# Attention weights' sums in an attention and mixture-of-experts kernel: last full key tile summed by TensorE, narrow pieces added two key tiles at once on GpSimd

## The chip, the core and the metric

The kernel runs on one core of one Trainium2 chip. The metric is device time in microseconds of one execution. TensorE does the matrix products (PE in the profile; PEld is its loading of weights), VectorE is DVE, ScalarE is ACT, GpSimd is POOL, and SyncE (SP) issues the DMAs.

## What is computed

There are 4 batches of 8 heads, 768 queries and keys a head, 64 dimensions. A query sees only the keys of its own cluster. The output of attention goes through 8 experts, with gates that are normalised 8 times over rows and columns.

```python
mask = q_assign[:, :, :, None] == k_assign[:, :, None, :]
scores = scale * np.matmul(q, k.transpose(0, 1, 3, 2))
scores = np.where(mask, scores, -1000000000.0)
scores = scores - np.max(scores, axis=-1, keepdims=True)
attn = np.exp(scores)
attn = attn / (np.sum(attn, axis=-1, keepdims=True) + 1e-09)
out = np.matmul(attn, v)
...
for e in range(E):
    h = np.maximum(x @ w1[e], 0.0)
    out += P[:, e:e + 1] * (h @ w2[e])
```

The change concerns `np.sum(attn, axis=-1)`, the sums by which the weights are divided.

## The kernel before

The kernel has two stages: attention, to about 530 us of the trace, and the experts, from there to the end at 2337.6 us. Heads are worked on in 16 pairs. The weights of a head lie with keys on the 128 partitions and queries along the row. There are six key tiles of 128 keys, and the 768 queries are cut at `N0` = 512. `CHUNKS` lists nine chunks a head, in three groups of three: key tile u with queries 0 to 511, key tile u+1 with queries 0 to 511, and then both key tiles with queries 512 to 767, side by side in one 512-wide tile. Chunk 7 (`NCH - 2`) is the last key tile with queries 0 to 511; chunk 8 is the last of all.

For each chunk, `max_chunk` (TensorE, line 733, then a VectorE maximum, line 737) and `max_rows` find the rows' maxima. In `max_rows` the maxima are rounded and split by ScalarE and GpSimd (lines 753 to 761), transposed on TensorE (line 766), copied by ScalarE (line 771) and moved by DMA into the operands of the next products. `exp_chunk` computes the scores on TensorE (lines 803 and 804, two PSUM buffers), and ScalarE turns them into the weights `pe` (line 810), in a ring of `PB` = 14 buffers. GpSimd then adds the weights into `psum`, a running sum over key tiles (line 829): ten adds a head, five of them 512 wide and five 256 wide. `values` multiplies the weights with V (line 862). `norm`, once a pair, adds `psum` up over the partitions with four products by ones (line 900), each into its own strip of 32 PSUM partitions, takes reciprocals and scales the output.

All products of lines 862, 900 and 1004 are in float32, and each leaves two matmul records in the trace.

The order of all engines' instructions is set by a planner when the program is built. Processes such as `exp_chunk` yield an engine and an estimated cost; the planner picks the next by key and start, and every engine then runs its instructions in that order. Tokens stand for buffers: `t_pe` has `PB` of them, and `release` gives one back when the add of a chunk (`ev["s", n, c]`) and its product with V are planned. Some steps may go to either of two engines: `split_part` subtracts (line 609) on VectorE or GpSimd, and one step of `assign_pair` (line 647) likewise. The experts' stage is planned apart, after attention. Its preparation of weights starts while the last pair is still under way (lines 1228 to 1251, 1353).

Of the kernel before, what the change touches and what calls it, by code (L numbers as in the profile page):

```python
# [8 lines left out]
F32 = mybir.dt.float32  # L9
# [5 lines left out]
ALU = mybir.AluOpType  # L15
# [7 lines left out]
P = 128  # L23
# [137 lines left out]
def attn_moe_kernel(  # L161
# [11 lines left out]
    nc = tc.nc  # L173
    B, H, S, D = q.shape
# [7 lines left out]
    SCALE = 1.0 / float(D) ** 0.5  # L182
    G = 4
    NA, NB = 3, 4
    PB = 14
    N0 = 512
    SPANS = ((0, N0), (N0, S))

# [12 lines left out]
    ones = const.tile([P, P], F32, name="ones")  # L201
# [11 lines left out]
    Q = 32  # L213
# [11 lines left out]
    PE, ACT, DVE, POOL, SP = "PE", "ACT", "DVE", "POOL", "SP"  # L225
# [114 lines left out]
    with ExitStack() as actx:  # L340
        nat = actx.enter_context(tc.tile_pool(name="nat", bufs=2))
        brief = actx.enter_context(tc.tile_pool(name="brief", bufs=1))
        work = actx.enter_context(tc.tile_pool(name="work", bufs=2))
# [27 lines left out]
        ps = misc_tile()  # L371
# [17 lines left out]
        bufs = {nm: [] for nm in NSET}  # L389
# [60 lines left out]
        NCH = len(CHUNKS)  # L450
# [56 lines left out]
        heads = {}  # L507
# [278 lines left out]
        def exp_chunk(n, c):  # L786

            p, y = divmod(n, 2)
            yield ev["rows", n]
            for to in (("qH", "kL"), ("kH", "qL"))[y]:  # L790
                yield ev["cross", p, to]
            if c:
                yield ev["begun", n, c - 1]
            yield t_s
            yield PE, 0.436, 0.107, 0.213
            t = heads[n]
            ev["begun", n, c].set(plan)
            i0, ni, a, z = CHUNKS[c]
            ps = ps_s.tile([P, 512], F32, name="exp_ps")
            for x in range(ni):  # L800
                ki = slice((i0 + x) * P, (i0 + x + 1) * P)
                o = ps[:, x * (z - a) : (x + 1) * (z - a)]
                nc.tensor.matmul(o, t["k1"][:, ki], t["q1"][:, a:z], start=True, stop=False)  # L803
                nc.tensor.matmul(o, t["k2"][0:98, ki], t["qa"][0:98, a:z], start=False, stop=True)  # L804
            if c == NCH - 1:
                ev["e", n].set(plan)
            yield t_pe
            yield ACT, 0.5
            pe = t["pe", c] = work.tile([P, ni, z - a], F32, name="pe", bufs=PB)
            nc.scalar.activation(pe, ps.rearrange("p (x c) -> p x c", x=ni), AF.Exp, scale=SCALE)  # L810
            t_s.put(plan)
            ev["p", n, c].set(plan)

            if c == 0:
                yield t_sum
                t["sum"] = work.tile([P, S], F32, name="psum", bufs=4)
                t["add"] = {}
            st, old = t["sum"], t["add"]
            if ni == 1:
                parts = [pe[:, 0]]  # L820
            else:
                parts = [pe[:, 0], pe[:, 1]]
            for part in parts:
                if a not in old:
                    old[a] = part
                    continue
                n_ = z - a
                yield POOL, 0.09 + n_ * 0.0019
                nc.gpsimd.tensor_tensor(out=st[:, a:z], in0=old[a], in1=part, op=ALU.add)  # L829
                old[a] = st[:, a:z]  # L830
            ev["s", n, c].set(plan)

        def release(p, c):

# [53 lines left out]
        def norm(p):  # L888
# [2 lines left out]
            b, h = divmod(n, H)  # L891
            for x in range(2):
                yield ev["s", n + x, NCH - 1]
            yield t_norm
            yield t_x
            yield PE, 0.75, 0.107, 0.64
            HS = S // 2
            ps = misc_tile()
            for g in range(4):
                nc.tensor.matmul(  # L900
                    ps[g * Q : (g + 1) * Q, 0:HS], ones[:, 0:Q], heads[n + g // 2]["sum"][:, g % 2 * HS : (g % 2 + 1) * HS], start=True, stop=True
                )
            for x in range(2):
                t_sum.put(plan)
            yield ACT, 0.48
            sc = work.tile([P, HS], F32, name="sc")
# [835 lines left out]
```

## Time and profile before

| | us |
|---|---|
| median of 3 runs (2338.98 to 2342.15) | 2341.17 |
| the profiled execution | 2339.39 |
| its span in the trace | 2337.6 |
| TensorE busy over the span | 2267.1 |
| GpSimd busy over the span | 1431.6 |
| VectorE busy over the span | 1873.1 |

The profile's page gives busy time by engine over the whole span, but the stages differ, so windows by stage are read beside it. A row of a group gives its line, engine, operation, tiles and shapes, its count, its busy time, the mean of one, and the idle time of the engine before it with what ended that. The chain of waits is followed back from the last instruction: at each step to what released it. A busy TensorE counts a matmul to the modelled end of its pipeline, so it isn't the same as a TensorE that streams at its peak.

### The profile page before, as it was taken

Reading aid. Unit: us, or ns where it says so; the run is one execution under the profiler, and the core shown is the slowest. Engines: PE = TensorE matmul, PEld = TensorE weight load, DVE = VectorE, ACT = ScalarE, POOL = GpSimd, SP = SyncE. Lnnn points to the kernel's source line nnn. Section 1 sums busy time; section 2 is a strip of 40 time slices with the busy share of each in tenths; the row PEclk is TensorE's granted clock in tenths of the full one; section 3 lists DMA queues with packets and bytes.
Section 4 is the critical chain, followed back from the end, with each engine's and each line's share of the span. In section 5 each row is a group of like instructions: output and inputs, shape, how many; then the busy total and the mean of one; then the engine's idle time right before and its main releaser. Section 6 shows DMA issues by size and latency. Waiting matters only on the chain.

```text
span 2337.6 us, 43307 instructions
## 1 busy us (share of the span) xinstructions
PE 2267.1 (97%) x16244; PEld 1611.5 (69%) x16244; DVE 1873.1 (80%) x3586; ACT 1155.6 (49%) x2313; POOL 1431.6 (61%) x1452
## 2 busy tenths in 40 slices
PE   7999999986999999999999999999999999999999
PEld 4555556543667777777777777777777777777777
DVE  7787777758988897789778877887797789777776
ACT  4555555565555554445444454545354545444432
POOL 4777888888846674646555573748274746556432
PEclk7999999997999999999999999999999999999999
DMA  6554454424424252243415242623252343414142
GB/s 162 138 143 112 101 126 100 123 96 169 145 94 147 84 167 87 93 140 111 131 49 176 86 142 61 199 83 114 84 168 79 101 129 122 131 49 131 50 141 82
DMA packets 172659, 271.49 MB, mean 116 GB/s; under 512 B 62904, under 2 KB 98848, under 8 KB 171936
## 3 DMA queue, kind: packets, MB, share of 16 engines
q1 hardware_dynamic: 172448, 268.72, 38.3%
q8 instruction: 127, 2.08, 0.4%
q14 instruction: 84, 0.69, 0.1%
HBM read 216.19 MB, written 23.59 MB: 103 GB/s over the span
## 4 chain that ended last, share of the span: by engine, by line
PE 85%; DVE 7%; POOL 3%; ACT 1%; issue 1%; DMA 1%; SPq 0%; DVEq 0%; ACTq 0%; POOLq 0%
PE a_ps L1434 20%; PE a_ps L1617 14%; PE ac_ps L1617 12%; PE c_ps L1617 10%; PE c_ps L1434 10%; PE b_ps L1434 5%; PE av_ps L862 4%; PE max_ps L733 3%; PE exp_ps L803 2%; POOL psum L829 2%; PE exp_ps L804 2%; DVE mrt L737 2%; PE misc_ps L591 1%; DVE vsum L542 1%; PE misc_ps L900 1%
## 5 line engine op out<-in xcount | busy, mean ns | idle before, releaser
L1617 PEld LDWEIGHTS <-h 128*128 128x128 f16 x8064 | 789.9, 98 | 198.2 <-issue 14.1
L1434 PEld LDWEIGHTS <-wa 128*128 128x128 f16 x5376 | 526.9, 98 | 281.1 <-issue 25.2
L1474 POOL TENSOR_TENSOR h<-s,h 128x384 f16<-128x384 f32 x126 | 126.0, 1000 | 530.0 <-ACT h L1472 527.6
L1463 ACT ACTIVATE h<-c 128x384 f16<-128x384 f32 x384 | 200.4, 522 | 436.0 <-DVE c L1457 434.4
L1617 PE MATMUL a_ps<-wb,h 128*128 128x256 f16 x3072 | 377.2, 273 | 3.4 <-DVE acc L1651 1.4
L1617 PE MATMUL ac_ps<-wb,h 128*128 128x256 f16 x2688 | 366.7, 273 | 2.6 <-DVE acc L1651 1.9
L1657 DVE SCALAR_TENSOR_TENSOR acc<-a_ps,gates,acc 128x256 f32<-128x256 f32 x472 | 220.7, 479 | 93.2 <-PE a_ps L1617 91.1
L1617 PE MATMUL c_ps<-wb,h 128*128 128x256 f16 x2304 | 284.9, 274 | 4.6 <-DVE acc L1653 3.4
L829 POOL TENSOR_TENSOR psum<-psum,pe 128x512 f32<-128x512 f32 (+1 forms) x256 | 265.8, 1058 | 36.9 <-ACT pe L810 30.1
L1474 POOL TENSOR_TENSOR h<-c,h 128x384 f16<-128x384 f32 x253 | 247.2, 989 | 48.7 <-ACT h L1472 39.8
L1465 DVE SCALAR_TENSOR_TENSOR h<-c,h 128x384 f16<-128x384 f32 x384 | 259.3, 678 | 5.1 <-ACT h L1463 5.0
L737 DVE TENSOR_REDUCE mrt<-max_ps 128x1 f32<-128x512 f32 (+1 forms) x288 | 189.9, 683 | 45.2 <-PE max_ps L733 43.5
L1657 DVE SCALAR_TENSOR_TENSOR acc<-ac_ps,gates,acc 128x256 f32<-128x256 f32 x412 | 197.1, 479 | 35.0 <-PE ac_ps L1617 32.6
L1657 DVE SCALAR_TENSOR_TENSOR acc<-c_ps,gates,acc 128x256 f32<-128x256 f32 x352 | 159.4, 478 | 79.3 <-PE c_ps L1617 78.8
L810 ACT ACTIVATE pe<-exp_ps 128x512 f32<-128x512 f32 x288 | 165.3, 596 | 96.5 <-PE exp_ps L804 70.4
L1454 ACT ACTIVATE c<-a_ps 128x384 f32<-128x384 f32 x256 | 124.9, 488 | 154.0 <-PE a_ps L1434 153.2
L1472 ACT CAST h<-c 128x384 f16<-128x384 f32 x256 | 128.1, 509 | 81.2 <-DVE c L1548 80.7
L1474 POOL TENSOR_TENSOR h<-h,h 128x384 f16<-128x384 f32 x125 | 141.8, 1134 | 35.7 <-PE c_ps L1617 23.9
L862 PE MATMUL av_ps<-pe,vn 128*64 128x512 f32 (+1 forms) x768 | 137.2, 500 | 0.0
L733 PE MATMUL max_ps<-kX,qX 96*128 96x256 f32 (+1 forms) x384 | 123.6, 388 | 8.0 <-DVE mrt L737 5.1
L804 PE MATMUL exp_ps<-qX,kX 98*128 98x256 f32 (+1 forms) x384 | 126.5, 342 | 0.0
L1454 ACT ACTIVATE h<-a_ps 128x384 f32<-128x384 f32 x128 | 62.7, 490 | 118.0 <-PE a_ps L1434 118.0
(478 smaller groups left out, 3938.6 us busy)
## 6 DMA issues: line engine op xcount, KB each, us to landing
raw<-in_moe_w SPq DMA_DIRECT2D x120, 512.0 KB
qn<-in_q SPq DMA_DIRECT2D x16, 384.0 KB
kn<-in_k SPq DMA_DIRECT2D x16, 384.0 KB
vn<-in_v SPq DMA_DIRECT2D x8, 768.0 KB
qX<-qH SPq DMA_DIRECT2D x32, 192.0 KB
kX<-kH SPq DMA_DIRECT2D x32, 192.0 KB
xd<-xT SPq DMA_DIRECT2D x4, 1536.0 KB
xqB<-xd SPq DMA_DIRECT2D x16, 384.0 KB
```

The source lines that it names most:

```text
L733: nc.tensor.matmul(ps[:, y * (z - a) : (y + 1) * (z - a)], t["qa"][0:96, i * P : (i + 1) * P], t["k2"][0:96, a:z], start=True, stop=True)
L737: nc.vector.tensor_reduce(out=t["mr"][:, i0 : i0 + ni, ni - 1], in_=ps.rearrange("p (x c) -> p x c", x=ni), axis=AX, op=ALU.max)
L804: nc.tensor.matmul(o, t["k2"][0:98, ki], t["qa"][0:98, a:z], start=False, stop=True)
L829: nc.gpsimd.tensor_tensor(out=st[:, a:z], in0=old[a], in1=part, op=ALU.add)
L862: nc.tensor.matmul(av[o, a:z], vn[:, i, :], heads[t]["pe", c][:, i - i0], start=(i == 0), stop=False, skip_group_check=True)
L1434: nc.tensor.matmul(ps[:, 0:HB], wt[:, w_, a, c, :], xv[:, x_, c, :], start=(n in (0, 1, 5) and s_ == 0), stop=(s_ == len(steps) - 1), skip ...
L1454: nc.scalar.activation(t, ps[:, 0:HB], func, scale=KAPPA)
L1463: nc.scalar.activation(t[:, 0], c, AF.Relu)
L1465: nc.vector.scalar_tensor_tensor(out=t[:, 1], in0=c, scalar=0.0, in1=t[:, 0], op0=ALU.max, op1=ALU.subtract)
L1474: by(w).tensor_tensor(out=t[:, 1], in0=c, in1=t[:, 0], op=ALU.subtract)
L1617: nc.tensor.matmul(view(m, i), t[:, a_, i * P : (i + 1) * P], w[:, b_, x, :], start=(opens and n == 0 and i in (0, 2)), stop=(n == 5), ski ...
L1657: nc.vector.scalar_tensor_tensor(out=to, in0=src, scalar=gate[b, e][:, ti : ti + 1], in1=to, op0=ALU.mult, op1=ALU.add)
```

## The change

Three things change. Chunks of the narrow kind (queries 512 to 767 of two key tiles) are no longer added as two 256-wide pieces, but as one 512-wide piece, so that `psum` grows to 1024 columns, of which the last 512 hold two partial sums side by side. Chunk 7 is no longer added on GpSimd at all: `norm` adds it with products of its own, from the weights themselves. So a head has six 512-wide adds in place of ten, and a pair has 12 products by ones in place of 4, with twice the columns in each strip of 32 partitions. `PB` goes from 14 to 12 to make room for the wider `psum`, and the buffer of chunk 7 is given back only after `norm`'s products.

```diff
-    PB = 14
+    PB = 12
...
-                t["sum"] = work.tile([P, S], F32, name="psum", bufs=4)
+                t["sum"] = work.tile([P, N0 + 2 * (S - N0)], F32, name="psum", bufs=4)
...
-            if ni == 1:
-                parts = [pe[:, 0]]
-            else:
-                parts = [pe[:, 0], pe[:, 1]]
-            for part in parts:
+            for part in [pe.rearrange("p x c -> p (x c)")] * (c != NCH - 2):
...
-                n_ = z - a
+                n_ = ni * (z - a)
                 yield POOL, 0.09 + n_ * 0.0019
-                nc.gpsimd.tensor_tensor(out=st[:, a:z], in0=old[a], in1=part, op=ALU.add)
-                old[a] = st[:, a:z]
-            ev["s", n, c].set(plan)
+                nc.gpsimd.tensor_tensor(out=st[:, a : a + n_], in0=old[a], in1=part, op=ALU.add)
+                old[a] = st[:, a : a + n_]
+            if c != NCH - 2:
+                ev["s", n, c].set(plan)
...
-            yield PE, 0.75, 0.107, 0.64
+            yield PE, 1.4, 0.107, 1.3
...
             for g in range(4):
-                nc.tensor.matmul(
-                    ps[g * Q : (g + 1) * Q, 0:HS], ones[:, 0:Q], heads[n + g // 2]["sum"][:, g % 2 * HS : (g % 2 + 1) * HS], start=True, stop=True
-                )
+                t, (a, z) = heads[n + g // 2], (g % 2 * HS, (g % 2 + 1) * HS)
+                own = []
+                if a < N0:
+                    m = min(z, N0)
+                    own = [(t["sum"][:, a:m], a, m), (t["pe", NCH - 2][:, 0, a:m], a, m)]
+                if z > N0:
+                    m, L = max(a, N0), S - N0
+                    own += [(t["sum"][:, y + m : y + z], m, z) for y in (0, L)]
+                for i, (v_, fa, fz) in enumerate(own):
+                    nc.tensor.matmul(
+                        ps[g * Q : (g + 1) * Q, fa - a : fz - a], ones[:, 0:Q], v_,
+                        start=(i == 0), stop=(i == len(own) - 1), skip_group_check=True,
+                    )
             for x in range(2):
+                ev["s", n + x, NCH - 2].set(plan)
                 t_sum.put(plan)
```

On TensorE, at the end of the last pair, the products by ones stood so before, between the last products with V and the transposes of the sums (line 911):

```order
L862 MATMUL av_ps<-pe,vn 64x512 x4
L862 MATMUL av_ps<-pe,vn 64x256 x4
L870 MATMUL av_ps<-nht_202,ve 128x512
L870 MATMUL av_ps<-nht_202,ve 128x256
L900 MATMUL misc_ps<-psum,ones 32x384 x4
L911 MATMUL misc_ps<-ident,sc 128x128 x3
```

Now, at the same place, where line 907 is the products by ones and 859, 867 and 920 are the lines around them:

```order
L867 MATMUL av_ps<-nht_202,ve 128x256
L907 MATMUL misc_ps<-psum,ones 32x384
L907 MATMUL misc_ps<-pe,ones 32x384
L907 MATMUL misc_ps<-psum,ones 32x128
L907 MATMUL misc_ps<-pe,ones 32x128
L907 MATMUL misc_ps<-psum,ones 32x256 x2
L907 MATMUL misc_ps<-psum,ones 32x384
L907 MATMUL misc_ps<-pe,ones 32x384
L907 MATMUL misc_ps<-psum,ones 32x128
L907 MATMUL misc_ps<-pe,ones 32x128
L907 MATMUL misc_ps<-psum,ones 32x256 x2
L920 MATMUL misc_ps<-ident,sc 128x128 x3
```

The first two go to the first strip of 32 partitions, the next four to the second, and so on: products of one strip now stand behind each other, where each had a strip of its own before.

On GpSimd, in the middle of attention, this stood before between the roundings of the maxima of two heads that follow each other (line 755; 756 and 761 belong to it):

```order
L755 TENSOR_SCALAR mm_195<-mr_2426 128x6
L756 TENSOR_TENSOR mm_195<-mr_2426,mm_195 128x6
L829 TENSOR_TENSOR psum<-psum,pe 128x512
L761 TENSOR_SCALAR flags_214<-mr_2426 128x6
L829 TENSOR_TENSOR psum<-psum,pe 128x512
L829 TENSOR_TENSOR psum<-psum,pe 128x256 x4
L829 TENSOR_TENSOR psum<-psum,pe 128x512 x2
L755 TENSOR_SCALAR mm_196<-mr_2543 128x6
```

And now, between the same two heads' roundings (the adds are line 825):

```order
L755 TENSOR_SCALAR mm_195<-mr_2410 128x6
L756 TENSOR_TENSOR mm_195<-mr_2410,mm_195 128x6
L761 TENSOR_SCALAR flags_214<-mr_2410 128x6
L825 TENSOR_TENSOR psum<-psum,pe 128x512 x3
L825 TENSOR_TENSOR psum<-pe 128x512 x2
L755 TENSOR_SCALAR mm_196<-mr_2564 128x6
```

Eight adds between the two roundings have become five.

At the end of attention, the first steps of the experts' weights (lines 1243, now 1252) stood on GpSimd behind 16 of the last pair's 20 adds; the last rows were:

```order
L829 TENSOR_TENSOR psum<-psum,pe 128x512
L829 TENSOR_TENSOR psum<-psum,pe 128x256
L1243 TENSOR_TENSOR sums<-raw 128x256
L1243 TENSOR_TENSOR sums<-sums,raw 128x256
L1243 TENSOR_TENSOR sums<-raw 128x256 x2
L829 TENSOR_TENSOR psum<-psum,pe 128x512
L829 TENSOR_TENSOR psum<-psum,pe 128x256 x3
L1251 TENSOR_TENSOR wa<-raw,wa 128x256
```

Now they begin behind 3 of the last pair's 12 adds:

```order
L825 TENSOR_TENSOR psum<-pe 128x512 x2
L825 TENSOR_TENSOR psum<-psum,pe 128x512
L1252 TENSOR_TENSOR sums<-raw 128x256
L1252 TENSOR_TENSOR sums<-sums,raw 128x256
L825 TENSOR_TENSOR psum<-psum,pe 128x512
L1252 TENSOR_TENSOR sums<-raw 128x256
L825 TENSOR_TENSOR psum<-psum,pe 128x512
L1252 TENSOR_TENSOR sums<-raw 128x256
L825 TENSOR_TENSOR psum<-psum,pe 128x512
L825 TENSOR_TENSOR psum<-pe 128x512 x2
L825 TENSOR_TENSOR psum<-psum,pe 128x512 x4
L1260 TENSOR_TENSOR wa<-raw,wa 128x256
```

The planner has also moved twelve of the subtractions of line 609 from GpSimd to VectorE (GpSimd had 32 and has 20: three 512 wide and nine 256 wide fewer), three steps of line 647 from VectorE to GpSimd, and three casts from ScalarE to VectorE. From the first product of the experts' stage to the end, TensorE's order is the same as before.

## Rows read from the trace of the kernel before

**Rows 1.** The page: busy time by engine; the chain that ended last.

```profile
PE 2267.1 (97%) x16244; PEld 1611.5 (69%) x16244; DVE 1873.1 (80%) x3586; ACT 1155.6 (49%) x2313; POOL 1431.6 (61%) x1452
...
PE 85%; DVE 7%; POOL 3%; ACT 1%; issue 1%; DMA 1%; SPq 0%; DVEq 0%; ACTq 0%; POOLq 0%
```

**Rows 2.** Windows by stage: length, then each engine's busy us, granted clock, DMA.

```profile
60.00:490.00 430.00, 418.44 (x2421) 247.93 (x2419) 321.32 (x575) 239.32 (x509) 343.08 (x403) 1.00 0.46 114
490.00:530.00 40.00, 33.59 (x171) 15.86 (x168) 14.66 (x21) 25.03 (x43) 35.38 (x37) 0.91 0.49 173
...
560.00:700.00 140.00, 120.44 (x867) 86.36 (x868) 131.72 (x264) 76.42 (x150) 95.82 (x85) 0.95 0.37 124
700.00:2330.00 1630.00, 1628.21 (x12490) 1221.89 (x12489) 1329.43 (x2574) 770.08 (x1530) 907.58 (x870) 1.00 0.36 112
```

**Rows 3.** Groups by line and shape, 40 to 540 us: the adds and subtractions.

```profile
L829 POOL TENSOR_TENSOR psum<-psum,pe 128x512 f32<-128x512 f32 x128 | 165.8, 1304 | 28.1 <-ACT pe L810 24.3 <-ACT mm L753 1.1 <-ACT mt L771 0.5
...
L829 POOL TENSOR_TENSOR psum<-psum,pe 128x256 f32<-128x256 f32 x128 | 102.2, 811 | 8.7 <-ACT pe L810 5.8
...
L829 POOL TENSOR_TENSOR psum<-pe 128x512 f32<-128x512 f32 x32 | 42.2, 1317 | 39.7 <-ACT pe L810 39.4
...
L829 POOL TENSOR_TENSOR psum<-pe 128x256 f32<-128x256 f32 x32 | 25.5, 806 | 6.2 <-ACT pe L810 6.0
...
L609 DVE TENSOR_TENSOR kL<-kn,kH 128x512 fp32r<-128x512 f32 x8 | 8.1, 1012 | 0.1
...
L609 DVE TENSOR_TENSOR qL<-qn,qH 128x256 fp32r<-128x256 f32 x3 | 2.4, 792 | 0.0
```

**Rows 4.** TensorE's timeline at the first pair's sums: start, length, line, tiles, count.

```profile
76.31 0.85 PE L900 MATMUL misc_ps<-psum,ones 128*32 128x384 f32 x8
77.09 0.74 PE L733 MATMUL max_ps<-kX,qX 96*128 96x512 f32 x3
```

**Rows 5.** TensorE's timeline at two other groups of products in strips.

```profile
70.26 0.51 PE L627 MATMUL misc_ps<-qn,cm 128*32 128x384 f32 x1
70.27 0.51 PE L627 MATMUL misc_ps<-kn,cm 128*32 128x384 f32 x1
...
70.61 0.49 PE L627 MATMUL misc_ps<-qn,cm 128*32 128x384 f32 x1
...
326.85 1.93 PE L1004 MATMUL misc_ps<-xT,wg 128*32 128x256 f32 x24
328.71 0.73 PE L733 MATMUL max_ps<-kX,qX 96*128 96x512 f32 x3
```

**Rows 6.** The chain of waits, 40 to 490 and 490 to 545 us: shares, longest pieces.

```profile
by line: PE av_ps L862 18.5%; PE max_ps L733 13.4%; PE exp_ps L803 10.7%; PE exp_ps L804 8.9%; POOL psum L829 8.3%; DVE mrt L737 7.2%; PE misc_ps L591 3.3%; issue 2.7%; DVE vsum L542 2.5%; PE misc_ps L900 2.4%; PE misc_ps L956 1.9%; ACT pe 
...
202.75 6.50 POOL psum L829 x7
...
by line: POOL psum L829 24.3%; issue 9.3%; ACT pe L810 7.4%; PE misc_ps L1004 6.7%; DMA xqB<-xd 6.2%; POOL xqB L328 5.1%; PE misc_ps L900 4.6%; PE c_ps L1434 3.8%; PE a_ps L1434 3.5%; POOL sums L1243 2.9%; DVE sums L1282 2.7%; PE exp_ps L80
```

**Rows 7.** Waits, 40 to 530 us: who waited for whom, total us, times, longest.

```profile
ACT mt L771 <- PE misc_ps L766: 24.5, 16, 2.7
PEld exp_ps L803 <- ACT pe L810: 14.4, 34, 1.5
...
ACT pe L810 <- POOL psum L829: 11.6, 7, 3.8
...
PEld misc_ps L766 <- POOL mm L756: 4.7, 5, 1.7
```

**Rows 8.** GpSimd's timeline at the end of attention.

```profile
498.66 3.48 POOL L829 TENSOR_TENSOR psum<-pe 128x512 f32<-128x512 f32 x2 [0.26 <-ACT pe L810]
502.10 11.60 POOL L829 TENSOR_TENSOR psum<-psum,pe 128x512 f32<-128x512 f32 x11
```

**Rows 9.** TensorE's timeline at the end of attention: gaps in brackets with what ended them.

```profile
506.30 0.39 PE L803 MATMUL exp_ps<-qL,kH 128*128 128x256 f32 x1 [1.07 <-ACT pe L810]
...
520.58 0.83 PE L900 MATMUL misc_ps<-psum,ones 128*32 128x384 f32 x2 [0.82 <-POOL psum L829]
```

More of the change, by code (lines that the diff above doesn't have):

```diff
@@ L893, in norm @@
                 yield ev["s", n + x, NCH - 1]
+                yield ev["p", n + x, NCH - 2]
             yield t_norm
             yield t_x
-            yield PE, 0.75, 0.107, 0.64
+            yield PE, 1.4, 0.107, 1.3
             HS = S // 2
```

## The prediction

> **What bounds the kernel now.** I read the page first, then windows by stage, then the chain of waits and the waits of the attention stage, and last the timelines at the places where the adds stand on the chain. The page says that TensorE is busy for 97% of the span and carries 85% of the chain, GpSimd 3% [rows 1]. That is an average over two stages. From 700 us on TensorE is busy 1628.21 of 1630 us, and from 560 to 700 us VectorE is busy 131.72 of 140 [rows 2]. The change touches neither, and TensorE's order there is the old one, so whatever attention gains or loses reaches the end unchanged. I look for the result before 530 us alone.
>
> From 60 to 490 us TensorE is busy 418.44 of 430 us, GpSimd 343.08, VectorE 321.32 [rows 2]. So TensorE bounds attention too, but narrowly: it idles 11.6 us there, and its in-order queue hides short waits in the ends of matmuls. GpSimd comes next, at 80%. The chain from 40 to 490 us runs through the adds for 8.3% of the time, and from 490 to 545 us for 24.3% [rows 6]: 0.083 x 450 = 37 us and 0.243 x 55 = 13 us. At 202.75 us seven adds stand in a row on it, ahead of the rounding of a head's maxima, for which TensorE waits. The question is thus whether freeing the second engine is worth more than loading the first.
>
> **The change, part by part.**
>
> GpSimd loses work. Before, all 320 adds take 165.8 + 102.2 + 42.2 + 25.5 = 335.7 us [rows 3]. After, each head has two first adds, which read two weight tiles (chunks 1 and 5), and four that read `psum`, all 512 wide: 64 x 1.317 + 128 x 1.304 = 251 us. That is 84.5 us less, or 5.3 us a pair. It is free only where GpSimd is waited for.
>
> TensorE gains work. A pair's sums took 0.78 us from their first start to the next instruction, 77.09 - 76.31, in eight records [rows 4]. Each strip of 32 partitions had 384 columns; now each has 768: 384 + 384 in the first and third, 128 + 128 + 256 + 256 in the second and fourth. What this costs depends on whether strips still run beside each other when the products of one strip stand behind each other in the queue. At 70.26 us products by line 627 stand in the order q, k, q, k, each with two records. Their first records start within 0.02 us, and the second records 0.35 us after them [rows 5]: the second half of the first product didn't hold up the first half of the next strip's. At 326.85 us 24 records of 256 columns in three strips are through in 1.86 us (328.71 - 326.85), eight rounds of 0.23 us [rows 5]. One record after another would take 24 x 0.23 = 5.6 us. So a blocked strip lets others pass, for at least the one or two products that stand there. I take strips side by side: the extra 384 columns a strip cost two more records of 0.35 us, +0.70 us a pair, 16 x 0.70 = +11.2 us, nearly all of it on the path, since TensorE has so little idle time. No row shows three products of a strip queued ahead of another strip; if strips then ran one by one, the price is the second rival's.
>
> The Trainium skill says otherwise: "TensorE: Matmul & The Clock Gate", Part 3 (packing small matmuls), has matmuls start and end in program order, with only weight loads pulled ahead. By that the four strips would hardly overlap, as in the second rival. The starts at 70.26 us [rows 5] speak against it, but they show a shallower queue than the new one.
>
> What freeing GpSimd gives back in the steady part (60 to 490 us) no row states. Its lower bound is nothing: TensorE is already 97% busy, and twelve subtractions move to VectorE, 3 x 1.012 + 9 x 0.792 = 10 us more there [rows 3]. Its upper bound is the idle 11.6 us, or more if waits hidden in matmul ends go too. The waits that a queue of adds can cause are: TensorE for the rounded maxima, 4.7 us in 5 times, ScalarE for weight buffers that an add still holds, 11.6 us, then TensorE for ScalarE's exponentials, 14.4 us, and ScalarE for the transposes behind the rounding, 24.5 us [rows 7]. They overlap, and most of what ScalarE waits never reaches TensorE. I take 7 us, over half the idle time, since the adds fall by a quarter and the eight adds between two roundings shown in the order become five.
>
> At the end of attention GpSimd is the bound. From 498.66 us it adds almost without a gap, 11 adds in 11.60 us from 502.10 on [rows 8]; TensorE meanwhile waits 1.07 us for exponentials and at 520.58 us 0.82 us for the last adds [rows 9]. The last pair's adds shrink by the 5.3 us above. Nothing back is the lower bound, 5.3 us the upper; I take 5.3, because GpSimd hardly pauses there. The steps of the experts' weights that now stand ahead of most of these adds take GpSimd's time at another place, not more of it; I cost that move at nothing, covered by VectorE, which is busy only 14.66 of 40 us there [rows 2].
>
> The ring of 12 `pe` buffers: what waits is ScalarE's exponential, behind which its whole queue stands, and then TensorE. Chunk 7's buffer is now held until the sums, chunk 2's until the add of chunk 5. Against that, GpSimd runs less behind. I cost it at nothing; its cover is the slack of GpSimd, and without it the third rival follows.
>
> Sum: +11.2 - 7 - 5.3 = -1.1 us against the profiled execution, 2339.39 us, so 2338.3 us; I say 2338. That execution lies 1.8 us under the median of the runs shown, 2341.17. The bounds of this case: steady part 0 to 11.6 back, the end 0 to 5.3 back, give 2339.4 + 11.2 - 16.9 = 2334 to 2351; as its own range I take 2331 to 2346, as both ends together are unlikely and some hidden waits may go.
>
> About 0.2%, 4.7 us, is what a measurement of this kernel can tell from no change: below 2336.5 is faster, above 2345.9 slower.
>
> **The rivals.**
>
> First, faster: GpSimd's queue is the true pace. The chain holds 37 + 13 = 50 us of adds [rows 6], more than TensorE's idle time, because a late rounding or buffer delays a whole head and TensorE fills in with other work that is due later. If half of these 50 us go, 2339.4 + 11.2 - 25 = 2325 us; if all, 2300. For it: GpSimd's 343 of 430 us and the seven adds in a row. Against: TensorE's 97%.
>
> Second, much slower: strips don't run side by side when their products queue behind each other. Then a product of 384 columns takes 0.70 us, of 256 0.46 and of 128 0.23, and only the last record of a strip overlaps the next strip's first: some 4.5 us a pair where it was 0.78, 3.7 x 16 = +60 us, and with the same 12.3 us back 2387 us. It decides as soon as a strip's first record starts after the strip before it has ended. Against it stand the starts at 70.26 and the 1.86 us at 326.85 [rows 5]; for it only that the queue ahead is longer.
>
> Third, slower: twelve buffers are too few. ScalarE's wait for buffers that adds hold, 11.6 us now [rows 7], doubles, passes to TensorE through the two score buffers, and eats what GpSimd gives back: 2339.4 + 11.2 = 2351 us. It decides where that wait grows past some 20 us. Against it: the adds now cost GpSimd 5.3 us a pair less, so buffers are freed sooner.
>
> **How the numbers follow.** Forecast 0.44 (faster 0.14, same 0.24, slower 0.06), first rival 0.27 (all faster), second 0.10 (all slower), third 0.19 (same 0.02, slower 0.17). So faster 0.41, same 0.26, slower 0.33. The range goes from 2316, into the first rival's far half, to 2360, past the third's; it leaves out the second (0.10) and perhaps 0.07 at the fast end.
>
> **What would show it.** In the changed kernel's profile: adds of 250 us in 192; GpSimd near 260 us busy in the same 430; the products by ones 1.4 to 1.6 us from first start to next instruction, with the second strip starting beside the first (else the second rival); the chain's share of adds from 40 to 490 us well under 8.3%, and TensorE's idle time there some 5 us; attention's last products by ones within a few us of 520.58; ScalarE's wait for adds not above 11.6 us (else the third rival). The forecast is wrong at its root if the time past 700 us moves, or if the pairs come closer together by over 1 us each, which TensorE's 97% doesn't allow without hidden waits.

## The result

The changed kernel takes 2351.81 us (median of 7 runs, 2347.27 to 2358.42) where the kernel before takes 2341.2 us (7 runs, 2338.98 to 2343.22): 10.6 us more, a ratio of 1.005 with a 95% interval of 1.0035 to 1.0065. It is slower, by more than the 0.2% that counts here, and 13.8 us above the 2338 forecast. It lies inside the range, but on the other side. The execution that was profiled took 2357.73 us, 6 us over the median of its seven, so its trace holds somewhat more than there is to explain on average; where that lies is said below. One run of e_fewer (2391.56 us) and one of the kernel before (3841.72 us) lie far above the others of their kernels and are left out of the differences below.

The page of the kernel after: busy time by engine, then the chain that ended last (they answer to [rows 1]).

```profile
PE 2289.5 (97%) x16500; PEld 1635.9 (69%) x16500; DVE 1877.1 (80%) x3598; ACT 1154.7 (49%) x2310; POOL 1338.5 (57%) x1315
...
PE 88%; DVE 7%; DMA 1%; issue 1%; ACT 1%; POOL 1%; SPq 1%; DVEq 0%; ACTq 0%; POOLq 0%
```

Windows by stage of the kernel after, in the columns of [rows 2]: length, busy us of PE, PEld, DVE, ACT, POOL, granted clock, DMA.

```profile
60.00:490.00 430.00, 419.94 (x2542) 257.56 (x2539) 310.81 (x562) 228.30 (x487) 245.05 (x266) 0.98 0.46 114
490.00:530.00 40.00, 37.79 (x204) 22.09 (x202) 22.97 (x34) 26.73 (x49) 27.79 (x28) 0.96 0.25 83
...
700.00:2330.00 1630.00, 1627.77 (x12467) 1219.63 (x12466) 1332.75 (x2574) 784.29 (x1562) 915.12 (x875) 1.00 0.35 111
```

GpSimd fell from 343 to 245 us busy in 60 to 490 us. TensorE is as full as it was: it idles 10.1 us there, where it idled 11.6. The experts' stage is the old one. So it is attention that got longer. The adds by shape (they answer to [rows 3]; the columns are busy us, mean ns, idle time before them):

```profile
L825 POOL TENSOR_TENSOR psum<-psum,pe 128x512 f32<-128x512 f32 x128 | 165.9, 1307 | 62.9 <-ACT pe L810 54.3 <-ACT mm L753 6.0 <-ACT rt L948 0.9
...
L825 POOL TENSOR_TENSOR psum<-pe 128x512 f32<-128x512 f32 x64 | 83.6, 1314 | 101.2 <-ACT pe L810 88.7 <-DMA qX<-mt 5.0 <-DMA nht<-mt 5.0
```

165.9 + 83.6 = 249.5 us in 192 adds: the relief of GpSimd is what the change promised, 86 us. ScalarE's wait for adds, 11.6 us in [rows 7], is down to 0.4 us. GpSimd is the one that waits, from 40 to 530 us (the list's first row: total us, times, longest), and the adds are gone from the chain of 40 to 490 us, where [rows 6] had 8.3%:

```profile
POOL psum L825 <- ACT pe L810: 142.9, 65, 8.6
```

```profile
by line: PE av_ps L859 20.8%; PE max_ps L733 14.7%; PE exp_ps L803 12.3%; PE exp_ps L804 10.2%; PE misc_ps L907 6.3%; DVE mrt L737 4.5%; PE misc_ps L591 3.5%; issue 2.1%; PE misc_ps L627 2.1%; PE misc_ps L965 2.0%; DMA rrow<-rt 1.7%; ACT pe
```

TensorE's timeline at the first pair's sums of the kernel after (answers to [rows 4]; start, length, line, tiles, count):

```profile
74.79 0.51 PE L907 MATMUL misc_ps<-psum,ones 128*32 128x384 f32 x3
75.04 0.27 PE L907 MATMUL misc_ps<-pe,ones 128*32 128x128 f32 x1
...
75.46 0.49 PE L907 MATMUL misc_ps<-pe,ones 128*32 128x384 f32 x1
...
75.78 0.49 PE L907 MATMUL misc_ps<-pe,ones 128*32 128x384 f32 x1
...
75.94 0.49 PE L907 MATMUL misc_ps<-pe,ones 128*32 128x384 f32 x1
...
76.26 0.49 PE L907 MATMUL misc_ps<-pe,ones 128*32 128x384 f32 x1
...
76.70 0.50 PE L733 MATMUL max_ps<-kX,qX 96*128 96x512 f32 x1
```

The burst lasts 76.70 - 74.79 = 1.91 us from its first start to the next instruction; before it was 0.78. That is +1.13 us a pair, +18.1 us for 16 pairs, where the prediction had +0.70 and +11.2. Why, the rows with 384 columns of chunk 7's weights (`pe`) show. The first head's two records start at 75.46 and 75.78, the second head's at 75.94 and 76.26: 0.48 us later. The strips of one head run side by side, but the second head's begin only when the first head's are partly through. Fourteen of the sixteen bursts are 1.91 us long; one at half clock takes 3.59, and behind the last one TensorE waits for ScalarE.

The first and the last burst start at 74.79 and 538.49 us, 463.7 us apart; before, at 76.31 and 517.62, 441.3 us apart. Fifteen bursts account for 17.0 of the 22.4 us. The clock adds to it in this execution (columns as in the windows above):

```profile
131.00:134.00 3.00, 1.74 (x8) 0.86 (x6) 1.50 (x4) 2.59 (x6) 1.30 (x1) 0.96 0.61 146
...
134.00:144.00 10.00, 9.91 (x42) 6.81 (x43) 5.03 (x9) 3.12 (x8) 3.96 (x4) 0.50 0.28 73
...
290.80:294.20 3.40, 3.40 (x16) 1.47 (x14) 2.19 (x4) 1.65 (x4) 2.20 (x2) 0.50 0.27 60
```

And TensorE's timeline at the start of that stretch:

```profile
131.63 0.46 PE L965 MATMUL misc_ps<-rrow,pick 4*128 4x512 f32 x1 [0.43 <-DMA rrow<-rt]
...
134.09 1.22 PE L733 MATMUL max_ps<-kX,qX 96*128 96x512 f32 x2 [0.93 <-DMA kX<-ot]
```

TensorE is busy 1.74 of the 3 us from 131 to 134, waiting for two transfers, and then 10 us are granted at 0.50 of full speed, the 1.2 GHz level. With three stretches of 3.4 us that makes 20 us at half clock between 60 and 490 us; before there were 3.4 us. Half of the difference, some 8.5 us, is time. Without it this execution would take some 2349 us, less than the median, so part of these stretches seems to belong to this execution and part to the kernel's order: the runs e_relief and e_alternate below, in the same order, show 11 and 10 us of half clock between 60 and 490 us, and in both 6.8 us of it begin at 134 us.

### The profile page after: what moved, and what is told of

Read it like the earlier page. It is cut to its first block, busy times and chain, and to the rows that moved or that the text cites. A ratio compares the mean times of both kernels' runs of the same rounds, so it can differ in the third digit from the quotient of the medians.

```text
span 2355.9 us, 43609 instructions
## 1 busy us (share of the span) xinstructions
PE 2289.5 (97%) x16500; PEld 1635.9 (69%) x16500; DVE 1877.1 (80%) x3598; ACT 1154.7 (49%) x2310; POOL 1338.5 (57%) x1315
## 4 chain that ended last, share of the span: by engine, by line
PE 88%; DVE 7%; DMA 1%; issue 1%; ACT 1%; POOL 1%; SPq 1%; DVEq 0%; ACTq 0%; POOLq 0%
PE a_ps L1443 20%; PE a_ps L1626 14%; PE ac_ps L1626 12%; PE c_ps L1626 10%; PE c_ps L1443 10%; PE b_ps L1443 5%; PE av_ps L859 5%; PE max_ps L733 3%; PE exp_ps L803 3%; PE exp_ps L804 2%; PE misc_ps L907 1%; DVE mrt L737 1%; PE misc_ps L591 1%; DVE h L1474 1%; DMA kn<-in_k 1%
## 5 line engine op out<-in xcount | busy, mean ns | idle before, releaser
L825 POOL TENSOR_TENSOR psum<-psum,pe 128x512 f32<-128x512 f32 x128 | 165.9, 1307 | 62.9 <-ACT pe L810 54.3
L825 POOL TENSOR_TENSOR psum<-pe 128x512 f32<-128x512 f32 x64 | 83.6, 1314 | 101.2 <-ACT pe L810 88.7
L804 PE MATMUL exp_ps<-qX,kX 98*128 98x512 f32 (+1 forms) x384 | 128.0, 346 | 0.0
```

The source lines that it names most:

```text
L825: nc.gpsimd.tensor_tensor(out=st[:, a : a + n_], in0=old[a], in1=part, op=ALU.add)
```

## The experiments

Twelve kernels were run, each beside the kernel before on the same chip (2341.17, 2340.50 and 2341.55 us in three groups). Differences below are those of the medians. The theory after the result was: TensorE pays the burst in full, and GpSimd's relief is worth less than the load.

**The two terms apart.** Run e_load keeps the kernel before and its order on TensorE and GpSimd, and gives TensorE the changed kernel's shapes; the repeats overwrite.

```diff
             for g in range(4):
-                nc.tensor.matmul(
-                    ps[g * Q : (g + 1) * Q, 0:HS], ones[:, 0:Q], heads[n + g // 2]["sum"][:, g % 2 * HS : (g % 2 + 1) * HS], start=True, stop=True
-                )
+                for f, l in ((0, HS), (0, HS)) if g % 2 == 0 else ((0, 128), (0, 128), (128, 256), (128, 256)):
+                    o = g % 2 * HS + f
+                    nc.tensor.matmul(
+                        ps[g * Q : (g + 1) * Q, f : f + l], ones[:, 0:Q], heads[n + g // 2]["sum"][:, o : o + l],
...
```

> Kernel before, with its order and its GpSimd adds untouched; only each pair's four products by ones are issued as 12 (384 twice in the first and third strip, 128, 128, 256, 256 in the second and fourth; each repeat overwrites the first, so the sums stay the same). It prices TensorE's added work alone. Theory (the burst takes 1.91 us where it took 0.78, and TensorE has no room for it): +1.13 x 16 = +18 us, 2359 us (2355 to 2362), clock as before. The price of the prediction (+0.70 a pair): 2352 us. Rival (TensorE has slack that hides the burst, and the changed kernel is slow for its new order or the ring of 12): 2341 to 2346 us.

Measured: 2355.54 us, +14.4, ratio 1.0061 (1.0048 to 1.0073). TensorE's timeline of that run at the first pair:

```profile
77.46 1.98 PE L902 MATMUL misc_ps<-psum,ones 128*32 128x384 f32 x24
79.37 0.74 PE L733 MATMUL max_ps<-kX,qX 96*128 96x512 f32 x3
```

The burst is 1.91 us here too, with every add still on GpSimd. Of its 18.1 us, 14.4 reach the end: four fifths.

Run e_relief is the opposite: the changed kernel in its own order, with the burst cut to the old four products.

```diff
-                    own = [(t["sum"][:, a:m], a, m), (t["pe", NCH - 2][:, 0, a:m], a, m)]
-                if z > N0:
-                    m, L = max(a, N0), S - N0
-                    own += [(t["sum"][:, y + m : y + z], m, z) for y in (0, L)]
+                    own = [(t["sum"][:, a:z], a, z)]
+                else:
+                    own = [(t["sum"][:, a:z], a, z)]
```

> Kernel after, with its order, its 192 adds and its ring of 12; only the products by ones are cut to four of 384 columns as in the kernel before (chunk 7's weights and the second narrow piece are left out of the sums, so the output is wrong by those). It prices the relief of GpSimd together with the new order, without TensorE's load. Theory (relief is worth something, the load eats it): 2351.8 - 18 = 2334 us (2329 to 2338), burst 0.78 us. Rival (GpSimd's adds never were the pace, the new order gives nothing): 2339 to 2343 us. Rival (the new order or the ring is itself slower): 2344 us or more.

Measured: 2333.85 us, -7.3, ratio 0.9963 (0.995 to 0.9977). With the burst back, 2351.81: 18 us more, as much as 16 bursts of 1.13 us take. The two runs settle the sign. In its own order the change is a relief worth 7 us and a load worth 18.

**Why the burst is 1.91 us.** Run e_alternate issues the same twelve products in turns over the strips; the order of everything else is that of the changed kernel.

```diff
-                for i, (v_, fa, fz) in enumerate(own):
-                    nc.tensor.matmul(
...
+                strips.append([(g, v_, fa - a, fz - a, i == 0, i == len(own) - 1) for i, (v_, fa, fz) in enumerate(own)])
+            for i in range(max(len(o) for o in strips)):
+                for o in strips:
+                    for g, v_, fa, fz, first, last in o[i : i + 1]:
+                        nc.tensor.matmul(
...
```

> Kernel after in the same order; only the 12 products by ones of a pair are issued in turns over the four strips (first products of strips 0, 1, 2, 3, then the second ones), not strip after strip. Theory (in the trace of after the strips of the second head start 0.48 us after those of the first, because only few products can wait ahead of them): all four strips start together, the burst falls from 1.91 to about 1.45 us, 0.46 x 16 = 7 us less, 2344.5 us (2341 to 2348). Rival (the burst is as long as its columns make it, whatever the order): 2351 to 2353 us, the burst 1.9 us.

Measured: 2345.35 us, +4.2, ratio 1.0019 (1.001 to 1.0028), 6.5 us less than the changed kernel. TensorE's timeline:

```profile
75.24 0.52 PE L911 MATMUL misc_ps<-psum,ones 128*32 128x384 f32 x6
...
75.91 0.50 PE L911 MATMUL misc_ps<-pe,ones 128*32 128x384 f32 x2
...
76.23 0.50 PE L911 MATMUL misc_ps<-pe,ones 128*32 128x384 f32 x2
...
76.68 0.50 PE L733 MATMUL max_ps<-kX,qX 96*128 96x512 f32 x1
```

Now the two heads' records of 384 columns start together (x2 at 75.91 and at 76.23), and the burst is 76.68 - 75.24 = 1.44 us, inside the 1.4 to 1.6 of the prediction. So the columns cost what was worked out; the order in which they were issued cost the other 0.47 us a pair, 7.5 us in all. With the burst that the prediction had in mind, the kernel is still slower than before: the burst alone doesn't make the miss.

**The relief at a fixed order.** Run e_fewer keeps the kernel before, its order on every engine and its burst, and leaves out 93 us of adds.

```diff
                 yield POOL, 0.09 + n_ * 0.0019
+                if c in (5, 7):
+                    continue
                 nc.gpsimd.tensor_tensor(out=st[:, a:z], in0=old[a], in1=part, op=ALU.add)
```

> Kernel before, same order on every engine, TensorE's products untouched; GpSimd leaves out three adds of each head (chunk 7's, 1.31 us, and both of chunk 5's, 0.80 us each: 93 us in all, the output lacks those weights in the sums). It prices GpSimd's relief at a fixed order. Theory (TensorE's idle time in the steady part, 10 to 12 us in every trace so far, isn't GpSimd's doing; only the wait of about 3 us ahead of the last sums is): 2337 us (2335 to 2339.5). Rival (what the prediction took, 7 us in the steady part and 5.3 at the end): 2329 us. Rival (GpSimd's queue is the pace): below 2325 us.

Measured: 2332.04 us (four runs), -9.5, ratio 0.9964 (0.9951 to 0.9978). It lies between the theory's 2337 and the prediction's 2329, nearer to the prediction: the theory of the moment was too low. Windows of that run, and TensorE's timeline at the rounded maxima near 210 us and at the last sums with the work behind them:

```profile
60.00:490.00 430.00, 421.32 (x2448) 249.82 (x2444) 313.30 (x574) 241.84 (x515) 261.96 (x322) 1.00 0.46 114
```

```profile
209.42 0.22 PE L766 MATMUL misc_ps<-ident_r,mm 128*18 128x128 f32 x1 [0.34 <-POOL mm L756]
...
513.02 0.85 PE L902 MATMUL misc_ps<-psum,ones 128*32 128x384 f32 x8
514.50 0.55 PE L913 MATMUL misc_ps<-ident,sc 128*128 128x128 f32 x3 [0.62 <-ACT sc L909]
```

The same places in the kernel before:

```profile
210.16 0.23 PE L766 MATMUL misc_ps<-ident_r,mm 128*18 128x128 f32 x1 [1.62 <-POOL mm L756]
...
517.62 0.83 PE L900 MATMUL misc_ps<-psum,ones 128*32 128x384 f32 x2
518.92 0.84 PE L900 MATMUL misc_ps<-psum,ones 128*32 128x384 f32 x4 [0.46 <-POOL psum L829]
520.58 0.83 PE L900 MATMUL misc_ps<-psum,ones 128*32 128x384 f32 x2 [0.82 <-POOL psum L829]
```

TensorE's idle time in 60 to 490 us falls from 11.6 to 8.7 us, and there is no half clock in that stretch. From the first burst (76.74) to the last it takes 436.3 us, 5.0 less than before. Of these, 2.8 us come by the sixth burst (148.1 us after the first, 150.9 before), where the wait for the rounded maxima falls from 1.62 to 0.34 us and 3.4 us at half clock behind it are gone. The run e_last below keeps that wait, shows no half clock behind it and takes 149.2 us, so some 1.7 us of the 2.8 hang on the clock. The last sums are issued without a gap, where before the adds held the last strip's product from 517.62 to 520.58 us, 2.96 us; from their first start to the end of the span it takes 3.0 us less. So in the profiled execution the steady part gives 5 us and the end 3. From 40 to 490 us the adds are gone from the list of the chain of that run: the 8.3% there, 37 us, turned into 5.

**Twelve buffers.** Run e_ring is the kernel before with a ring of 12; e_order12 has the order that belongs to a ring of 12, but 14 real buffers.

```diff
-    PB = 14
+    PB = 12
```

> Kernel before with 12 buffers for the weights instead of 14, and the order that the planner then makes; nothing else. Theory (the ring is no bound): 2338 to 2345 us, ScalarE's wait for adds at most some 15 us. Rival (twelve buffers hold ScalarE up, the third rival of the prediction): 2347 us or more, that wait over 20 us.

```diff
-        t_nat, t_sc, t_pe, t_nh, t_vn = Tokens(2), Tokens(1), Tokens(PB), Tokens(6), Tokens(2)
+        t_nat, t_sc, t_pe, t_nh, t_vn = Tokens(2), Tokens(1), Tokens(PB - 2), Tokens(6), Tokens(2)
```

> Kernel before in the order that the planner makes for a ring of 12 (word for word that of the run e_ring, 2348.35 us), but with 14 real buffers for the weights. Theory (the order is what cost e_ring its 7 us: two waits of 3.1 us at 66.8 and 135.0 us and the half clock behind them; no wait for buffers stands out there): 2346 to 2351 us, the same two waits. Rival (ScalarE is held up by the twelve buffers themselves): 2338 to 2343 us.

Measured: e_ring 2348.35 us, +7.2, ratio 1.0028 (1.0017 to 1.004); e_order12 2349.36 us, +8.9, ratio 1.003 (1.0019 to 1.0042). The two spare buffers bring nothing back, and ScalarE's wait for adds is 9.5 us in e_ring, so the buffers aren't what costs. It is the order that the planner makes for 12. TensorE's timeline of e_order12 at its two largest waits, then VectorE's and GpSimd's at the first:

```profile
62.91 0.70 PE L733 MATMUL max_ps<-kX,qX 96*128 96x512 f32 x3
66.89 0.80 PE L733 MATMUL max_ps<-kX,qX 96*128 96x512 f32 x1 [3.09 <-DVE mrt L737]
...
134.90 0.65 PE L956 MATMUL misc_ps<-rrow,pick 4*128 4x512 f32 x1 [2.47 <-DMA rrow<-rt]
```

```profile
63.15 0.42 DVE L609 TENSOR_TENSOR qL<-qn,qH 128x256 fp32r<-128x256 f32 x1
63.48 1.36 DVE L607 CAST kH<-kn 128x256 fp32r<-128x256 f32 x1
64.87 1.36 DVE L609 TENSOR_TENSOR kL<-kn,kH 128x256 fp32r<-128x256 f32 x1
66.16 1.27 DVE L737 TENSOR_REDUCE mrt<-max_ps 128x1 f32<-128x512 f32 x2
```

```profile
63.39 1.29 POOL L609 TENSOR_TENSOR kL<-kn,kH 128x512 fp32r<-128x512 f32 x1
64.65 2.71 POOL L829 TENSOR_TENSOR psum<-psum,pe 128x512 f32<-128x512 f32 x2
```

```profile
66.70:73.60 6.90, 6.71 (x18) 3.52 (x20) 2.89 (x6) 1.39 (x3) 4.03 (x7) 0.51 0.46 90
```

In this order a cast and a subtraction of 256 columns stand ahead of the maxima on VectorE, each takes 1.36 us, TensorE waits 3.09 us, and the next 6.9 us are granted at half clock. Behind the second wait, 2.47 us for a transfer, stand 6.8 us more; in all there are 17 us at half clock between 60 and 490 us, where before there were 3.4, and e_ring has the same 17. A third rival for the changed kernel, then, though not the one that was priced: not the buffers, but the order.

Run e_ring14 asks whether the changed kernel suffers from its ring of 12: e_alternate with 14 weight buffers and three tiles for the sums.

```diff
-    PB = 12
+    PB = 14
...
-                t["sum"] = work.tile([P, N0 + 2 * (S - N0)], F32, name="psum", bufs=4)
+                t["sum"] = work.tile([P, N0 + 2 * (S - N0)], F32, name="psum", bufs=3)
```

> Run e_alternate (2345.35 us) with 14 weight buffers and three tiles for the sums, not 12 and four, in the order that the planner makes for that. Theory (no buffer of the ring is waited for; only the order's accidents change): 2341 to 2349 us, attention's products by ones about as far apart as there (30.06 us). Rival (the ring of 12 costs the changed kernel what e_ring lost, 7 us): 2336 to 2340 us.

Measured: 2345.04 us, +4.5, ratio 1.0023 (1.0014 to 1.0032), the time of e_alternate. The ring isn't what holds the changed kernel back, as far as two runs with two orders can tell.

**Each part of the change alone.** e_chunk7 moves only chunk 7's sums to TensorE (ring of 14, products in turns, an order of its own); e_chunk7_same does so in the order of the kernel before; e_pieces only sets the narrow pieces side by side (ring of 12, products in turns, an order of its own).

```diff
 e_chunk7_same, against before
                 yield POOL, 0.09 + n_ * 0.0019
+                if c == NCH - 2:
+                    continue
...
-            for g in range(4):
-                nc.tensor.matmul(
+            for i in range(2):
+                for g in range(4):
+                    t, o = heads[n + g // 2], g % 2 * HS
+                    src, l = (t["sum"], HS) if i == 0 else (t["pe", NCH - 2][:, 0], min(HS, N0 - o))
+                    nc.tensor.matmul(
...
 e_pieces, against e_alternate
-            for part in [pe.rearrange("p x c -> p (x c)")] * (c != NCH - 2):
+            for part in [pe.rearrange("p x c -> p (x c)")]:
...
```

> Only one part of the change: chunk 7's weights are summed by TensorE, the narrow pieces are added one by one as before; ring of 14, products in turns over the strips (384 + 384 columns in the first and third strip, 128 + 128 + 256 in the others). Theory (TensorE pays for each column in full, +0.66 x 16 = 10.6 us, and the relief is worth some 5 us and only where attention ends): 2347 us (2343 to 2350), no better than e_alternate, since the burst is as long there. Rival (chunk 7 is the good part, and the ring and the side by side pieces spoil it): 2338 us or less.

> The one part of the change of run e_chunk7 (chunk 7's weights summed by TensorE, narrow pieces as before, ring of 14), but in the order of the kernel before on every engine. Theory (+0.64 x 16 = 10.3 us for TensorE, 3 to 4 us back at the end; that e_chunk7 came to 2342.1 us is its new order's luck): 2347.5 us (2345 to 2350). Rival (the relief itself is worth 9 us): 2341 to 2343 us.

> The other part alone: narrow pieces side by side (224 adds), chunk 7 added by GpSimd as before, ring of 12, products in turns: 384 columns in the first and third strip, 128 + 256 + 256 in the others. Theory (burst 1.2 to 1.3 us, +0.45 x 16 = 7 us, against 6 us of relief, with the order's accidents of 3 us either way): 2342 us (2339 to 2346). Rival (this part costs nothing on TensorE since the first and third strip stay at 384 columns and set the length): 2335 us.

Measured: e_chunk7 2342.14 us, +1.6, ratio 1.0008 (0.9999 to 1.0017); e_chunk7_same 2345.55 us, +4.0, ratio 1.0017 (1.0009 to 1.0026); e_pieces 2348.31 us, +6.8, ratio 1.0034 (1.0023 to 1.0046). Their bursts are 1.42, 1.42 and 1.22 us long. In the old order chunk 7's burst costs 0.64 x 16 = 10.2 us and 6.2 us come back for 42 us of adds. With a burst as long, e_chunk7 lies 2.4 us lower, each beside the kernel before on its chip; that may be its order, but the two intervals overlap. e_pieces costs 0.44 x 16 = 7.0 us and gets nothing back; its trace has waits of 1.38 and 1.69 us near 212 us and 6.8 us of half clock there (0.66, 1.62 and 3.4 us in the kernel before), so its order may have eaten part of the relief, but this part wasn't run in the old order, and its share stays open.

**The relief where it is waited for.** e_last and e_last2 keep the kernel before and its order, and let TensorE sum the weights of the last of the 16 pairs alone: chunk 7's, or chunks 7's and 8's.

```diff
+            ones_add = n // 2 == npairs - 1 and c == NCH - 2
-            for part in parts:
+            for part in parts * (not ones_add):
...
 e_last2
+            ones_add = n // 2 == npairs - 1 and c >= NCH - 2
```

> Kernel before, same order; only the last of the 16 pairs has chunk 7's weights summed by TensorE (four products more, two adds of 1.31 us fewer). Theory (GpSimd's adds are waited for at the end of attention alone, where TensorE stood 3.3 us for them ahead of its last sums): 2341.2 - 2.6 + 0.3 = 2339 us (2337 to 2340.5). Rival (what the relief gains, it gains in the steady part over all pairs): 2340.5 to 2342 us.

> Kernel before, same order; for the last of the 16 pairs alone TensorE sums the weights of chunks 7 and 8 itself (eight products more, six adds fewer). Theory (GpSimd leaves the end of the chain altogether: the 1.08 us that TensorE still waited for adds in run e_last, and a shorter way to them): 2338 us (2336.5 to 2339.3), 2.5 to 4 us under before. Rival (the exponentials end as late as the adds, and nothing more comes back): 2339 to 2340.5 us.

Measured: e_last 2339.3 us, -1.2, ratio 0.9992 (0.9984 to 1.0001); e_last2 2339.21 us, -2.3, ratio 0.999 (0.9981 to 0.9999). TensorE's timeline of e_last at the rounded maxima and at the last sums, then e_last2's last sums:

```profile
211.32 0.23 PE L766 MATMUL misc_ps<-ident_r,mm 128*18 128x128 f32 x1 [1.62 <-POOL mm L756]
...
518.45 0.51 PE L910 MATMUL misc_ps<-psum,ones 128*32 128x384 f32 x1 [1.08 <-POOL psum L830]
```

```profile
515.21 0.85 PE L918 MATMUL misc_ps<-psum,ones 128*32 128x384 f32 x8
515.88 1.26 PE L918 MATMUL misc_ps<-pe,ones 128*32 128x384 f32 x16
518.34 0.55 PE L934 MATMUL misc_ps<-ident,sc 128*128 128x128 f32 x3 [1.20 <-ACT sc L930]
```

e_last still waits 1.08 us for adds; in e_last2 no add stands at the end any more, and it pays for that with a longer burst. It is the one version here with all the sums that is faster than both kernels, by 0.1%, which is hardly more than the runs can tell. In the profiled executions 1.2 us of its gain lie ahead of the fifteenth burst (416.1 us after the first, 417.3 before), where nothing was changed and only the kernel before has a stretch at half clock. What the end alone gives is not shown by these two runs.

## Why the prediction was wrong, step by step

- **GpSimd's relief in its own time**: right. 192 adds, 249.5 us against the 250 expected, and 245 us busy against 260.
- **TensorE's term, +0.70 us a pair**: the first of two steps that failed. "I take strips side by side" rested on [rows 5], where the products of the strips are issued in turns or stand in one strip one or two deep. In the change six products of a head's two strips stand ahead of the second head's. The burst took 1.91 us and not 1.4 to 1.6, and 16 x 1.13 = 18.1 us stood where 11.2 were put, 6.9 us more. In turns it is 1.44 us (e_alternate), so the price of the columns was right. The sentence that "No row shows three products of a strip queued ahead" named the gap; the value was then taken from the end that the rows did show. The second rival, strips one by one, didn't come either: 4.5 us was its burst. The truth lay between the two, a case that the prediction didn't price. Why the second head's strips begin late at just that depth stays open: e_alternate shows that the order of issue decides it, not what holds them.
- **Against the Trainium skill's rule**: in the rows of the changed kernel the first strip's second product, `pe` with 384 columns, is issued ahead of the second strip's `pe` with 128; yet that one starts at 75.04 us and the former at 75.46. The Trainium skill ("TensorE: Matmul & The Clock Gate", Part 3, packing small matmuls) has matmuls start in program order, and these rows don't agree with that. The order of issue does matter, though, which I took it not to.
- **What freeing GpSimd gives back, 7 + 5.3 = 12.3 us**: the second step that failed, by 5 us. In the changed kernel's order it is 7.3 us (e_relief). Either miss alone turns the sign of the sum: 18.1 - 12.3 = +5.8, 11.2 - 7.3 = +3.9.
- **Steady part, 7 us back**: near the right size at a fixed order (e_fewer: 5 us in the trace for a little more relief, some 1.7 of them by the clock), less in the kernel as it is. Its TensorE waits for other things: `kX<-ot` 2.1 us where it was 0.6, `rrow<-rt` 2.0 us, with half clock behind them. The sign that was named, TensorE idle some 5 us in 60 to 490, did not appear: 10.1.
- **End of attention, 5.3 us back**: mis-sized. The end gives 3.0 us in the trace of e_fewer. How long GpSimd adds there was taken for what TensorE waits: in the kernel before, TensorE's own products run to 517.62 us, and the adds hold only the 2.96 us from there to 520.58. [rows 9] show the second of the two waits in these (0.82 us) and not the first (0.46). That the last products by ones start within a few us of 520.58 us failed too: they start at 538.49.
- **Ring of 12 at nothing**: right for the buffers (the wait of 11.6 us fell to 0.4, and e_ring14 changes nothing), so the third rival's mechanism fell. Its time, 2351 us, came true by other means: 2341.2 + 18.1 - 7.3 = 2352.0.
- **The first rival** (GpSimd's queue is the true pace, 25 to 50 us) fell: with 93 us of adds gone, 9.5 us came back. The chain's 37 + 13 us of adds were places through which the chain was followed, not time to be had.
- **What was not in the prediction**: that another ring makes the planner write another order, and that such an order alone can cost 7 to 9 us (e_ring, e_order12). The places in the prediction were read from the order; what it makes TensorE wait for was not priced.
- **The time past 700 us** did not move, as expected: TensorE is busy 1627.77 against 1628.21 us.

The sum with the measured terms: 2341.2 + 18.1 - 7.3 = 2352.0 us against 2351.8 measured. Both terms are those of the changed order. In the old order the burst costs 14.4 us (e_load) and the relief gives 9.5 back (e_fewer, for 93 us of adds), some 5 us together; why it is 10.6 in the changed order was not taken apart.

## What to carry to other kernels

Move work onto the engine that bounds a stage only if what it relieves is waited for by that engine: read who ends its idle time, not the share that the other engine has on the chain, and give no more back than the idle time holds. Products in column strips are to be issued in turns over the strips; a burst issued strip after strip overlapped here only in part, and such a burst is to be priced from rows of the same depth. Where a planner writes the order, run the new order with the old work first: here it was worth as much as the change.

## What the hardware showed that was not expected

- Column strips of TensorE overlap beyond the order of issue, but not without limit: with six products of one head issued ahead, the other head's strips began 0.48 us late (1.91 us a burst); issued in turns, all four ran together (1.44 us).
- VectorE's cast of 128x256 took 1.36 us at 63.48 in e_order12 and ended at 64.84, as GpSimd's subtraction (63.39 to 64.68) did; the subtraction behind it, 1.36 us too, ran beside GpSimd's adds. A subtraction of the same size, just before, with GpSimd mostly on small work, took 0.42 us. The same trace has both near 140 us, where GpSimd has no instruction from 139 to 142.5 us: there the cast took 0.28 us, a fifth, and the subtraction 0.42. The Trainium skill ("GPSIMD Engine Reference", section 1, specifications) has the two engines share their interfaces to SBUF, with contention in certain forms of VectorE's instructions; the rows agree with that, and no run here moved the one away from beside the other alone.
- A few us in which TensorE was partly idle were in places followed by 3.4 to 10 us at the 1.2 GHz level: 1.74 busy us of 3 ahead of 10 us at 0.50 in the changed kernel, an idle 3.09 us ahead of 6.9 us at 0.51 in e_order12. But the same wait doesn't always have it: 1.62 us for the rounded maxima stand ahead of 3.4 us at 0.51 in the kernel before (210.16) and ahead of 4 us at 1.00 in e_last (211.32), where the instructions are the same. A stretch at half clock in one trace is thus not by itself an effect of the kernel.

VectorE's timeline of e_order12 at 140 us, then the windows behind the wait of 1.62 us, in the kernel before and in e_last:

```profile
140.62 0.28 DVE L607 CAST kH<-kn 128x256 fp32r<-128x256 f32 x1
140.94 0.42 DVE L609 TENSOR_TENSOR kL<-kn,kH 128x256 fp32r<-128x256 f32 x1
```

```profile
211.60:215.00 3.40, 3.40 (x16) 1.34 (x12) 0.00 (x1) 0.49 (x1) 1.27 (x1) 0.51 0.28 61
```

```profile
212.00:216.00 4.00, 4.00 (x27) 1.63 (x25) 0.87 (x3) 1.34 (x3) 1.69 (x2) 1.00 0.30 67
```
